# Part of the weight decoding moved from VectorE to GpSimd, another order of the first phase, and a check split in two

## The chip, the cores and the metric

The kernel runs on one core of a Trainium2 chip. A core has TensorE (matrix products into PSUM), VectorE and ScalarE (elementwise work on SBUF and PSUM), GpSimd (elementwise work on SBUF, and DMAs that it issues itself), SyncE, which here issues most DMAs, and 16 DMA engines. The metric is the device time in microseconds. Each engine works through its instructions in the order in which they were issued to it and waits for others by semaphores.

## The reference

A gated linear attention over four batches and eight heads, followed by a two-layer network with a squared ReLU:

```python
f = 1 / (1 + exp(-f_logit))                       # B=4, H=8, S=768, D=48
for t in range(S):
    state = f[:, :, t, :, None] * state + einsum('bhd,bhe->bhde', k[:, :, t], v[:, :, t])
    y[:, :, t] = einsum('bhd,bhde->bhe', q[:, :, t], state)
x = y.transpose(0, 2, 1, 3).reshape(3072, 384)    # tokens x model
h = maximum(x @ w_in, 0)                          # w_in 384 x 2048
out = (h * h) @ w_out                             # w_out 2048 x 384
```

The two weights arrive as 64-bit floats.

## The kernel before, in words

**Tiling.** The 768 steps are six blocks of 128, the eight heads four pairs. A *unit* is one block and one pair of heads; it is numbered block by block, so units 0 to 3 are block 0 and units 4 to 7 block 1. The network's 2048 hidden rows are 16 *pieces* f of 128. Of each piece there are two weights, one of `w_in` (called i0, i1, ...) and one of `w_out` (o0, o1, ...), each 128x384.

**A unit** goes through small stages, each a method with one letter: L loads gates, keys and queries (f and k load them apart), v loads the values, G takes the sigmoid on ScalarE, K the key scan on VectorE (line 422), in which GpSimd makes two 128x8 rows (line 427) that the query scan needs, Q the query scan (436), T and N transpose the keys (472 on TensorE, 478 on ScalarE), D and S are the state and score products (496, 507), M masks the scores (514), C forms the states (529, 534), r and s are crossed copies for the other half (458, 466), Y the output products (550, 562), H and X split the outputs into an upper and a lower part (575, 579). Heads have 48 rows of 64; the fourth pair lives in the rows that the other three leave free. So m moves 16 rows of a unit (447), and g and h bring the fourth pair's outputs into the other three's tiles (586), partly issued by GpSimd, partly by SyncE.

**Two-part products.** TensorE's single pass is of reduced width, so each operand is kept as an upper part and a lower part, and each product is three passes (line 251 for the up-projection, 277 for the down-projection): upper weight by lower x, lower weight by upper x, upper by upper. Nine passes of 512 columns make one up- or down-projection of a piece.

**Decoding.** A weight is loaded as 64-bit words and made into a 32-bit float: an absolute value and, for the pieces loaded early, a byte taken out by ScalarE (144, 148), two bit operations on VectorE (154, 161), and then the two parts: a copy that rounds to the upper part on ScalarE (176) and the subtraction that leaves the lower part on VectorE (178). In the order below these are the letters A I V c J for `w_in` and B O Z d P for `w_out`. The first six pieces (12 weights) are decoded *early*; the other ten later, while block 1's products run. A 112x256 piece, called w4, serves the fourth pair in pieces 0 and 1 and has the letters e n t a w.

**Phases.** The first phase computes block 0's units, block 1's units and pieces 0 to 5 of block 0's network; u and U are up-projections (u without the fourth pair's part for pieces 0 and 1, U0 and U1 then add that part), R and E the squaring and its lower part, W the down-projection. Then come all 16 pieces of block 1, the other ten pieces of block 0, and blocks 2 to 5, each with the next block's units between its pieces.

**What sets the order.** In the first phase two strings of such letters, FIRST and SECOND, are run through one after the other; each letter issues its instructions at once, and for the engines named in `manual_schedule` that order is kept. Before, these are TensorE, SyncE, VectorE and ScalarE; GpSimd's instructions are placed by the scheduler. The letters i, o, L, v issue loads on SyncE's queue. A load into a buffer that is still in use waits there, and all behind it on that queue.

**The verdict.** The fast decoding and the scans hold for a range of values. Near the end a check over all gate products and weights is made (`verdict`): four VectorE rows, a transpose on TensorE, three more VectorE rows. Its flag is read in the last block and decides whether a general path runs; with these inputs it doesn't. It is issued behind piece 12 of the last block but one.

Of the kernel before, what the change touches and what calls it, by code (L numbers as in the profile page):

```python
# [12 lines left out]
F32 = mybir.dt.float32  # L13
# [7 lines left out]
ALU = mybir.AluOpType  # L21
ET = mybir.EngineType
# [43 lines left out]
VERDICT_AT = 12  # L66
# [1 line left out]
SIGNED = ()  # L68

FIRST = """  # L70
f0 k0 L1 G0 K0 v0 o4 L2 Q0 busy11 T0 G1 N0 o0 K1 m0 busy3 S0 B4 j0 D0 i1 M0 r0 T1 C0 v1 G2 Q1 v2 s0
o5 busy2 Y0 B0 i5 K2 e0 m1 S1 v3 H0 i0 r1 n0 N1 Q2 o3 T2 B5 D1 L4 O0 r2 S2 M1 N2 C1 A0 D2 m2 t0 X0
D3 a0 v4 C2 s1 i3 I0 s2 Y1 A1 w0 V0 L5 Z0 G4 I1 S3 M2 H1 V1 r3 L6 X1 c1 C3 Y2 A3 K4 s3 v5 c0 v6 H2
M3 T4 o2 G5 X2 N4 J0 i2 Y3 A5 Q4 i4 d0 u0 H3 v7 P0 m4 r4 o1 X3 G6 I3 J1 A2 D4 K5
"""
SECOND = """
U0 A4 S4 I2 R0 T5 C4 u1 M4 s4 E0 N5 V2 Q5 Y4 c2 g3 h3 B1 U1 H4 W0 J2 m5 r5 X4 O1 R1 V3 Z1 D5 I4 S5
d1 E1 B3 U2 P1 C5 c3 B2 M5 W1 J3 s5 V4 K6 R2 Y5 c4 Q6 T6 H5 U3 N6 X5 m6 r6 J4 D6 R3 E2 S6 O2 U4 C6
Z2 s6 M6 d2 E3 Y6 R4 P2 I5 W2 V5 H6 E4 c5 X6 r7 J5 S7 O3 D7 M7 U5 C7 Z3 s7 O4 d3 Y7 Z4 P3 d4 W3 H7
P4 R5 X7 O5 g7 h7 Z5 W4 E5 d5 P5 W5  # L80
"""


class Moe:
# [28 lines left out]
    def decode_fourth(self):  # L113
        a = self.const.tile([P, DM], F32, tag=self.spare(), name="wa4")[:ROWS, : SPLIT * P]
        yield from self.bits(self.raw4, a, None, "j0")
        w = self.const.tile([P, 2, DM], F32R, tag=self.fourth_tag, name="w4")
        self.w4 = w[:ROWS, :, : SPLIT * P]
        yield from self.halves(self.w4, a)

    def decode(self, f, i, scr, early):  # L120

        if early:
            a = self.const.tile([P, DM], F32, tag=self.spare(), name=f"wa{f}_{i}")
        else:
            a = scr.tile([P, DM], F32, tag="wa", name=f"wa{f}_{i}", bufs=3)
        total = self.sums[:, 2 * f + i : 2 * f + i + 1]
        yield from self.bits(self.raw[f, i], a, total, f"{'io'[i]}{f}" if early else None)
        yield from self.parts(f, i, a)

    def bits(self, st, a, total, early):  # L130

# [35 lines left out]
            )  # L167
        yield

    def parts(self, f, i, a):  # L170
        self.w[f, i] = self.const.tile([P, 2, DM], F32R, tag=f"w{f}_{i}", name=f"w{f}_{i}")
        yield from self.halves(self.w[f, i], a)

    def halves(self, w, a):
        nc = self.nc
        nc.scalar.copy(out=w[:, 0], in_=a)  # L176
        yield
        nc.vector.tensor_tensor(out=w[:, 1], in0=a, in1=w[:, 0].bitcast(F32), op=ALU.subtract)  # L178
# [158 lines left out]
def fast_path(ctx, tc, moe, ident, low, fkqT, vN, w, w4, out):  # L337
    nc = tc.nc
# [340 lines left out]
    moe.begin(0, xs[0], half[0])  # L679
    early = ExitStack()  # L680
    pro = early.enter_context(tc.tile_pool(name="pro", bufs=1))
    with tc.manual_schedule(engines={ET.PE, ET.SP, ET.DVE, ET.Activation}):
        with tc.tile_pool(name="ps_p", bufs=2, space=bass.MemoryType.PSUM) as ps_p:
            for t in FIRST.split():
                step(t)
# [51 lines left out]
        for blk in range(2, NBLK):  # L737
# [8 lines left out]
                hook(0, first + out_at, 1, lambda un=un, stage=out_stage: un.stage(stage))  # L746

        general = []
        hook(len(order) - 2, VERDICT_AT, 1, lambda: general.append(verdict(nc, moe, low, ident, ps_a)))
        hook(  # L750
            len(order) - 1, VERDICT_AT, 1,
            lambda: general.append(nc.values_load(general[0][0:1, 0:1], min_val=0, max_val=1)),
        )
        for k, (blk, fs) in enumerate(order):
            if blk > 1 and blk + 1 < NBLK:
# [8 lines left out]
            else:  # L764
                moe.run(hooks[k])
                moe.finish(lambda e: out[blk, e * P : (e + 1) * P], None if blk else part)
    return general[1], obs


def verdict(nc, moe, low, ident, pool):  # L770
# [6 lines left out]
    nc.vector.tensor_scalar(out=moe.sums, in0=moe.sums, scalar1=MOST, scalar2=None, op0=ALU.is_lt)  # L777
    nc.vector.tensor_reduce(out=good[:, 1:2], in_=moe.sums, axis=mybir.AxisListType.X, op=ALU.min)
    nc.vector.tensor_tensor(out=good[:, 0:1], in0=good[:, 0:1], in1=good[:, 1:2], op=ALU.min)
    pl = pool.tile([1, P], F32, tag="pk", name="pl")  # L780
    nc.tensor.transpose(out=pl, in_=good[:, 0:1], identity=ident)
# [186 lines left out]
```

## Time and profile before

| what | us |
|---|---|
| median of three runs | 510.5 (509.83 to 512.45) |
| the profiled execution | 511.15, span 509.4 |
| TensorE busy in the span | 490.5 |
| VectorE busy | 263.0 |
| ScalarE busy | 284.0 |
| GpSimd busy | 29.2 |
| first phase, to the end of its last down-projection on TensorE | 76.3 |
| in it: TensorE, VectorE, ScalarE busy | 65.0, 65.8, 53.2 |

The profile is of one execution. In its views a row has its start and duration in microseconds, the engine, the line of the kernel, the operation and the tiles (output<-inputs); in brackets stands how long the engine sat idle before it and what ended that. PE is TensorE, PEld its weight loads, DVE VectorE, ACT ScalarE, POOL GpSimd, SPq SyncE's queue.

### The profile page before, as it was taken

To read this page: it belongs to the slowest core of one execution; us is meant where nothing else is said; L and a number is where in the kernel's file an instruction comes from. 1 tells how busy PE (TensorE), PEld (TensorE's weight loads), DVE (VectorE), ACT (ScalarE), POOL (GpSimd) and SP (SyncE) were. 2 spreads that over 40 slices of the span, in tenths; PEclk is the share of its full clock that TensorE was granted. 3 is DMA by queue.
4 is the path that set the end of the run, shared out by engine and by line. 5 is a ranking of instruction groups with operands and counts; after the bars stand their busy time and mean duration, and the time that the engine had idled before them with its cause. 6 is when DMAs were issued, how large, how long until landed. Compare 5 with 4: busy or idle time off the path is not lost.

```text
span 509.4 us, 11456 instructions
## 1 busy us (share of the span) xinstructions
PE 490.5 (96%) x4831; PEld 391.3 (77%) x4831; DVE 263.0 (52%) x483; ACT 284.0 (56%) x577; POOL 29.2 (6%) x66
## 2 busy tenths in 40 slices
PE   5799899999999999999999999999999999999996
PEld 5677677788777878777788787778777767888884
DVE  6899975989857335645324546224455241211112
ACT  3789746887757353755354754543656444544441
POOL 6112010001000000000000000000000000000000
PEclk9999999999999999999999999999999999999999
DMA  8992025562530206112005313004410001100001
GB/s 293 312 317 51 13 79 171 178 207 97 166 90 18 74 11 178 73 27 89 3 1 150 110 28 90 0 1 119 141 28 12 1 1 33 64 0 1 0 1 67
DMA packets 20364, 41.97 MB, mean 82 GB/s; under 512 B 2656, under 2 KB 5728, under 8 KB 20304
## 3 DMA queue, kind: packets, MB, share of 16 engines
q1 hardware_dynamic: 19856, 40.23, 26.0%
q0 software_dynamic: 448, 0.92, 0.8%
q8 instruction: 40, 0.66, 0.5%
q14 instruction: 20, 0.16, 0.1%
HBM read 31.69 MB, written 4.72 MB: 71 GB/s over the span
## 4 chain that ended last, share of the span: by engine, by line
PE 78%; DVE 12%; ACT 4%; DMA 3%; issue 2%; POOL 0%; SPq 0%; DVEq 0%; ACTq 0%; POOLq 0%
PE ph L251 36%; PE po L277 33%; PE ds L507 2%; PE ds L496 2%; PE py L550 2%; PE py L562 2%; DVE fkq L436 1%; DMA last_kq<-fkq 1%; DVE gl L268 1%; DVE fkq L422 1%; DMA fkq<-in_fkqT_dram 1%; DVE wa L161 1%; PE pk L472 1%; ACT ph L262 1%; DVE w L178 1%
## 5 line engine op out<-in xcount | busy, mean ns | idle before, releaser
L251 PE MATMUL ph<-x,w 128*128 128x512 f32 x864 | 222.4, 402 | 1.2 <-DVE gl L268 0.7
L251 PEld LDWEIGHTS ph<-x,w 128*128 128x128 f32 x864 | 160.0, 189 | 39.2 <-DVE gl L268 1.1
L277 PE MATMUL po<-gh,w 128*128 128x512 f32 x576 | 180.4, 394 | 0.3 <-DVE w L178 0.3
L268 DVE TENSOR_TENSOR gl<-ph,gh 128x512 fp32r<-128x512 f32 x96 | 66.2, 690 | 187.9 <-ACT gh L263 187.7
L261 ACT ACTIVATE ph<-ph 128x512 f32<-128x512 f32 x96 | 55.8, 582 | 136.6 <-PE ph L251 135.9
L277 PEld LDWEIGHTS po<-gh,w 128*128 128x128 f32 x576 | 108.1, 188 | 26.6 <-DVE w L178 0.6
L277 PE MATMUL po<-gl,w 128*128 128x512 f32 x288 | 114.7, 398 | 0.4 <-DVE gl L268 0.4
L277 PEld LDWEIGHTS po<-gl,w 128*128 128x128 f32 x288 | 54.1, 188 | 13.7 <-DVE gl L268 1.1
L263 ACT CAST gh<-ph 128x512 fp32r<-128x512 f32 x96 | 56.3, 586 | 3.0
L262 ACT ACTIVATE ph<-ph 128x512 f32<-128x512 f32 x96 | 55.9, 582 | 3.0
L427 POOL TENSOR_SCALAR fkq<-fkq 128x8 f32<-128x8 f32 x18 | 11.8, 656 | 324.0 <-DVE fkq L422 323.9
L422 DVE TENSOR_TENSOR_SCAN fkq<-fz,dr 128x520 f32<-128x520 f32 x18 | 22.3, 1237 | 6.7 <-ACT fz L417 6.6
L176 ACT CAST w<-wa 128x384 fp32r<-128x384 f32 (+1 forms) x33 | 16.8, 510 | 13.9 <-DVE wa L165 12.2
L550 PEld LDWEIGHTS py<-sc,vn 64*64 64x64 f32 (+1 forms) x640 | 18.0, 126 | 8.1 <-issue 7.0
L436 DVE TENSOR_TENSOR_SCAN fkq<-fz,dz 128x520 f32<-128x520 f32 x18 | 22.4, 1242 | 0.6
L550 PE MATMUL py<-sc,vn 64*64 64x64 f32 (+1 forms) x640 | 21.3, 222 | 0.7 <-DVE sc L514 0.7
L562 PE MATMUL py<-rx,sx 48*48 48x64 f32 (+1 forms) x320 | 20.7, 217 | 0.2
L514 DVE TENSOR_TENSOR sc<-ds,mask 128x512 f32<-128x512 f32 x24 | 16.5, 687 | 8.2 <-PE ds L507 7.5
L144 ACT ACTIVATE wa<-raw 128x384 f32<-128x384 f32 (+1 forms) x33 | 18.1, 549 | 4.5 <-DMA raw<-in_w_dram 4.4
L161 DVE SCALAR_TENSOR_TENSOR wa<-raw,wa 128x384 int32<-128x384 int32 (+1 forms) x33 | 18.1, 552 | 0.8
L562 PEld LDWEIGHTS py<-rx,sx 48*48 48x48 f32 (+1 forms) x320 | 18.1, 127 | 0.5 <-ACT sx L466 0.5
L178 DVE TENSOR_TENSOR w<-wa,w 128x384 fp32r<-128x384 f32 (+1 forms) x33 | 18.0, 546 | 0.7 <-ACT w L176 0.6
(93 smaller groups left out, 403.0 us busy)
## 6 DMA issues: line engine op xcount, KB each, us to landing
fkq<-in_fkqT_dram SPq DMA_DIRECT2D x17, 768.0 KB, 5.2
raw<-in_w_dram SPq DMA_DIRECT2D x32, 384.0 KB, 4.3
vn<-in_vN_dram SPq DMA_DIRECT2D x24, 192.0 KB, 4.9
out_dram<-ob SPq DMA_DIRECT2D x12, 256.0 KB, 2.1
x<-ys SPq DMA_DIRECT2D x30, 64.0 KB, 2.4
last_kq<-fkq SPq DMA_DIRECT2D x28, 64.5 KB, 2.3
out_dram<-part SPq DMA_DIRECT2D x3, 256.0 KB, 2.4
out_dram<-ob_last SPq DMA_DIRECT2D x3, 256.0 KB, 2.4
```

What stands on the lines that cost most here:

```text
L161: nc.vector.scalar_tensor_tensor(out=h, in0=upper, scalar=-(1 << 31), in1=h, op0=ALU.bitwise_and, op1=ALU.bitwise_or)
L178: nc.vector.tensor_tensor(out=w[:, 1], in0=a, in1=w[:, 0].bitcast(F32), op=ALU.subtract)
L251: self.nc.tensor.matmul(self.ph[f], lhsT=w[:, i], rhs=x[:, j], start=first and n == 0, stop=last and n == 2)
L261: nc.scalar.activation(ph, ph, AF.Relu)
L262: nc.scalar.activation(ph, ph, AF.Square)
L263: nc.scalar.copy(out=gh, in_=ph)
L268: self.nc.vector.tensor_tensor(out=gl, in0=self.ph.pop(f), in1=gh.bitcast(F32), op=ALU.subtract)
L277: self.nc.tensor.matmul(self.po[e], lhsT=l, rhs=r, start=f == self.fs[0] and i == 0, stop=f == self.fs[-1] and i == 2,)
L422: V.tensor_tensor_scan(out=rr[:, ::-1], data0=self.fz[:, NZ * CZ : 0 : -1], data1=dr[:, ::-1], initial=0.0, op0=ALU.mult, op1=ALU.add,)
L436: V.tensor_tensor_scan(out=pp, data0=self.fz[:, : NZ * CZ], data1=dz, initial=0.0, op0=ALU.mult, op1=ALU.add)
L550: nc.tensor.matmul(self.py[h * C : h * C + m, c, b * C : (b + 1) * C], lhsT=self.vn[rows, b, h * D : h * D + m], rhs=self.sc[rows, h, b], ...
L562: nc.tensor.matmul(self.py[h * C : h * C + m, c, b * C : (b + 1) * C], lhsT=s[rows, b * D : b * D + m], rhs=q[rows], start=False, stop=b = ...
```

## The change

Three things. The lower parts of the 12 early weights are computed by GpSimd instead of VectorE; those of w4 and of the later weights stay on VectorE. GpSimd's instructions now keep the written order too, and both strings of the first phase are new ones. And the verdict is issued in two steps, the first four VectorE rows behind piece 12, the rest from the transpose on behind piece 13.

```diff
-f0 k0 L1 G0 K0 v0 o4 L2 Q0 busy11 T0 G1 N0 o0 K1 m0 busy3 S0 B4 j0 D0 i1 M0 r0 T1 C0 v1 G2 Q1 v2 s0
+f0 k0 L1 G0 K0 i2 v0 o3 Q0 busy11 T0 L2 G1 N0 K1 m0 busy3 S0 r0 A2 i0 D0 M0 B3 v3 T1 C0 v1 Q1 s0 i1
...
     def decode_fourth(self):
...
-        yield from self.halves(self.w4, a)
+        yield from self.halves(self.w4, a, self.nc.vector)
...
     def decode(self, f, i, scr, early):
...
-        yield from self.parts(f, i, a)
+        yield from self.parts(f, i, a, self.nc.gpsimd if early else self.nc.vector)
...
-    def halves(self, w, a):
+    def halves(self, w, a, eng):
         nc = self.nc
         nc.scalar.copy(out=w[:, 0], in_=a)
         yield
-        nc.vector.tensor_tensor(out=w[:, 1], in0=a, in1=w[:, 0].bitcast(F32), op=ALU.subtract)
+        eng.tensor_tensor(out=w[:, 1], in0=a, in1=w[:, 0].bitcast(F32), op=ALU.subtract)
         yield
...
-    with tc.manual_schedule(engines={ET.PE, ET.SP, ET.DVE, ET.Activation}):
+    with tc.manual_schedule(engines={ET.PE, ET.SP, ET.DVE, ET.Activation, ET.Pool}):
...
-        hook(len(order) - 2, VERDICT_AT, 1, lambda: general.append(verdict(nc, moe, low, ident, ps_a)))
+        found = verdict(nc, moe, low, ident, ps_a)
+        for n in range(2):
+            hook(len(order) - 2, VERDICT_AT + n, 1, lambda: general.append(next(found)))
         hook(
             len(order) - 1, VERDICT_AT, 1,
-            lambda: general.append(nc.values_load(general[0][0:1, 0:1], min_val=0, max_val=1)),
+            lambda: general.append(nc.values_load(general[1][0:1, 0:1], min_val=0, max_val=1)),
         )
...
     nc.vector.tensor_tensor(out=good[:, 0:1], in0=good[:, 0:1], in1=good[:, 1:2], op=ALU.min)
+    yield
     pl = pool.tile([1, P], F32, tag="pk", name="pl")
...
-    return flag
+    yield flag
```

The loads ahead of unit 4's inputs (L4) in the order of issue were f0 k0 L1 v0 o4 L2 o0 j0 i1 v1 v2 o5 i5 v3 i0 o3; now they are f0 k0 L1 i2 v0 o3 L2 i0 v3 v1 i1 v2 j0 L5 v4 o4 i3 o0 L6.

Three places of the new order, as the instructions stand on an engine. In their names the number behind a tile is the buffer's; the digit of the piece is left out, so `w_0` is a piece of `w_in` and `w_1` one of `w_out`. First TensorE around unit 3's outputs and u0; before:

```order
L550 MATMUL first_py<-sc_3_529,vn_3_307 48x64 x4
L562 MATMUL first_py<-last_kq,sp_76 48x64
L562 MATMUL first_py<-rx_3_481,sx_78 48x64
L251 MATMUL ph_0_156<-x_0_115,w_0_524 128x512 x3
L251 MATMUL ph_0_156<-x_1_116,w_0_524 128x512 x3
L251 MATMUL ph_0_156<-x_2_117,w_0_524 128x512 x3
```

and now:

```order
L507 MATMUL ds_3_439<-last_kq 64x64 x16
L251 MATMUL ph_0_156<-x_0_115,w_0_497 128x512 x3
L251 MATMUL ph_0_156<-x_1_116,w_0_497 128x512 x3
L251 MATMUL ph_0_156<-x_2_117,w_0_497 128x512 x3
L550 MATMUL first_py<-sc_3_543,vn_3_233 48x64 x4
L562 MATMUL first_py<-last_kq,sp_76 48x64
```

u0 now follows unit 3's scores at once; unit 3's outputs and unit 4's transpose, which stood between them, come behind it.

Then ScalarE at unit 2's crossed states (the copy of `sp_75` to `sx_77`) and the upper part of i0, in the new order:

```order
L417 ACTIVATE fz_73<-fkq_1_307 128x8x64
L176 CAST w_0_431<-wa_0_330 128x384
L144 ACTIVATE wa_1_435,sums<-raw_1_344 128x384
L148 ACTIVATE raw_1_344<-raw_1_344,floor 128x384
L466 COPY sx_77<-sp_75 48x208
L144 ACTIVATE wa_1_462,sums<-raw_1_384 128x384
L148 ACTIVATE raw_1_384<-raw_1_384,floor 128x384
L458 COPY rx_3_492<-last_kq 48x256
L176 CAST w_0_497<-wa_0_310 128x384
```

Unit 5's gates and the words of o4 (`raw_1_344`) now stand ahead of the crossed states, and those of o0 (`raw_1_384`) and unit 3's queries ahead of the upper part of i0 (`w_0_497`); before, the crossed states followed those of unit 1 directly.

Last, GpSimd from unit 1's move on, in the new order:

```order
L447 DMA last_kq<-fkq_1_140 16x1032 x2
L178 TENSOR_TENSOR w_0_431<-wa_0_330,w_0_431 128x384
L178 TENSOR_TENSOR w_0_497<-wa_0_310,w_0_497 128x384
L178 TENSOR_TENSOR w_1_521<-wa_1_462,w_1_521 128x384
L427 TENSOR_SCALAR fkq_0_458<-fkq_0_458 128x8
L427 TENSOR_SCALAR low<-fkq_0_458 128x8
L447 DMA last_kq<-fkq_0_458 16x1032 x2
```

Three lower parts stand between unit 1's move and unit 4's rows; two follow unit 5's rows of line 427 and seven unit 6's.

More of the change, by code (lines that the diff above doesn't have):

```diff
@@ L70 @@
 FIRST = """
-f0 k0 L1 G0 K0 v0 o4 L2 Q0 busy11 T0 G1 N0 o0 K1 m0 busy3 S0 B4 j0 D0 i1 M0 r0 T1 C0 v1 G2 Q1 v2 s0
-o5 busy2 Y0 B0 i5 K2 e0 m1 S1 v3 H0 i0 r1 n0 N1 Q2 o3 T2 B5 D1 L4 O0 r2 S2 M1 N2 C1 A0 D2 m2 t0 X0
-D3 a0 v4 C2 s1 i3 I0 s2 Y1 A1 w0 V0 L5 Z0 G4 I1 S3 M2 H1 V1 r3 L6 X1 c1 C3 Y2 A3 K4 s3 v5 c0 v6 H2
-M3 T4 o2 G5 X2 N4 J0 i2 Y3 A5 Q4 i4 d0 u0 H3 v7 P0 m4 r4 o1 X3 G6 I3 J1 A2 D4 K5
+f0 k0 L1 G0 K0 i2 v0 o3 Q0 busy11 T0 L2 G1 N0 K1 m0 busy3 S0 r0 A2 i0 D0 M0 B3 v3 T1 C0 v1 Q1 s0 i1
+N1 Y0 G2 v2 j0 K2 m1 r1 S1 L5 H0 A0 D1 X0 A1 M1 T2 v4 C1 o4 Q2 s1 e0 busy2 Y1 i3 N2 o0 n0 m2 r2 I1
+S2 H1 L6 V1 G5 X1 D2 c1 M2 B4 J1 D3 C2 L4 I0 s2 B0 I2 Y2 t0 V0 r3 O0 o1 c0 Z0 S3 H2 J0 V2 v6 d0 X2
+o2 A3 P0 C3 u0 i5 M3 G4 I3 a0 K4 o5 s3 B1 Y3 i4 Q4 B2 v5 T4 v7 H3
 """
 SECOND = """
[L77 to L80, printed above, removed]
+u1 N4 X3 m4 B5 O2 w0 O1 r4 Z2 U0 g3 h3 Z1 c2 U1 K5 R0 J2 S4 D4 G6 E0 T5 d1 C4 W0 N5 P1 M4 s4 Q5 R1
+Y4 U2 H4 E1 m5 r5 X4 V3 A4 K6 S5 D5 R2 W1 C5 c3 J3 M5 s5 T6 Q6 A5 Y5 U3 H5 m6 r6 X5 E2 d2 I4 N6 S6
+P2 V4 R3 D6 M6 W2 C6 c4 E3 s6 J4 O5 r7 Y6 Z5 I5 d5 U4 V5 H6 P5 c5 X6 J5 O3 Z3 S7 R4 O4 D7 Z4 U5 C7
+d4 d3 P4 M7 s7 E4 P3 R5 Y7 W3 H7 E5 X7 g7 h7 W4 W5
 """
@@ L168, in bits, with parts @@
         yield
-    def parts(self, f, i, a):
+    def parts(self, f, i, a, eng):
         self.w[f, i] = self.const.tile([P, 2, DM], F32R, tag=f"w{f}_{i}", name=f"w{f}_{i}")
-        yield from self.halves(self.w[f, i], a)
-    def halves(self, w, a):
+        yield from self.halves(self.w[f, i], a, eng)
+    def halves(self, w, a, eng):
         nc = self.nc
@@ L196, in decode_any @@
         )
-        for _ in self.parts(f, i, a):
+        for _ in self.parts(f, i, a, self.nc.vector):
             pass
@@ L766, in fast_path @@
                 moe.finish(lambda e: out[blk, e * P : (e + 1) * P], None if blk else part)
-    return general[1], obs
+    return general[2], obs
 def verdict(nc, moe, low, ident, pool):
```

## The prediction

> **What bounds the kernel now.** I read the page first: the busy shares, then the forty slices.
>
> ```profile
> span 509.4 us, 11456 instructions
> PE 490.5 (96%) x4831; PEld 391.3 (77%) x4831; DVE 263.0 (52%) x483; ACT 284.0 (56%) x577; POOL 29.2 (6%) x66
> PE   5799899999999999999999999999999999999996
> DVE  6899975989857335645324546224455241211112
> DMA  8992025562530206112005313004410001100001
> ```
>
> TensorE sets the time: 490.5 of 509.4 us, full in every slice but the first three and the last. So only its 18.9 idle us, and its slow-clock time, can be won. Where they lie, the view by stretches tells; the cuts are at the end of unit 3's scores, the first up-projection u0, and the end of the last down-projection of the first phase (column two is the stretch, three is TensorE, five VectorE; the last is GB/s).
>
> ```profile
> 0.00:28.26 28.26, 19.71 (x380) 16.65 (x380) 22.57 (x43) 16.89 (x40) 9.98 (x26) 1.00 0.97 305
> 28.26:34.05 5.79, 4.97 (x101) 4.22 (x101) 5.65 (x11) 5.17 (x14) 0.97 (x2) 1.00 0.88 297
> 34.05:37.95 3.90, 3.90 (x15) 2.86 (x16) 3.87 (x7) 3.28 (x8) 1.04 (x3) 1.00 0.96 348
> 42.70:69.97 27.27, 25.35 (x520) 19.76 (x519) 25.91 (x51) 20.78 (x49) 2.66 (x6) 1.00 0.13 26
> 100.00:410.00 310.00, 309.45 (x3164) 246.99 (x3163) 160.12 (x281) 174.11 (x348) 11.15 (x24) 1.00 0.25 72
> 410.00:422.00 12.00, 10.75 (x47) 8.38 (x46) 4.18 (x14) 4.48 (x9) 0.00 (x0) 1.00 0.01 2
> ```
>
> Until 38 us the loads run at 0.88 to 0.97 of the DMA engines; from 42.7 to 70 VectorE is at 25.91 of 27.27 and TensorE loses 27.27 - 25.35 = 1.92 us. From 100 to 410 there is nothing to win (0.55), from 410 to 422 there is 1.25. The change touches the first 76 us and that last place.
>
> Then the chain of waits through the first 42 us, and TensorE's and ScalarE's rows there.
>
> ```profile
> 19.28 7.47 DMA last_kq<-fkq
> 26.89 1.37 PE ds L507 x32
> 34.12 3.84 PE ph L251 x9
> 94.82 2.10 PE ph L251 x9
> ```
> ```profile
> 24.66 0.34 PE L562 MATMUL first_py<-rx,sx 48*48 48x64 f32 x1 [1.24 <-ACT sx L466]
> 24.89 0.56 ACT L144 ACTIVATE wa<-raw 128x384 f32<-128x384 f32 x1
> 25.45 0.62 ACT L148 ACTIVATE raw<-raw,floor 128x384 int32<-128x384 uint8 x1
> 25.96 0.68 PE L562 MATMUL first_py<-rx,sx 48*48 48x64 f32 x2
> 26.34 0.63 ACT L417 ACTIVATE fz<-fkq 128x512 f32<-128x512 f32 x1 [0.27 <-DMA fkq<-in_fkqT_dram]
> 42.70 0.34 PE L550 MATMUL py<-sc,vn 64*64 64x64 f32 x8
> 43.79 0.95 PE L251 MATMUL ph<-ys,w 112*128 112x512 f32 x3
> 54.05 0.66 PE L472 MATMUL pk<-ident,fkq 128*128 128x128 f32 x4 [0.63 <-DVE fkq L428]
> ```
>
> Unit 3's scores wait for the 7.47 us that unit 2's rows take in the loaded queue. The nine products of u0 take 3.84 us, those of a later up-projection 2.10: u0 runs at half the rate.
>
> **The change, part by part.** *The verdict.* These rows are its place.
>
> ```profile
> 417.88 0.69 DVE L268 TENSOR_TENSOR gl<-ph,gh 128x512 fp32r<-128x512 f32 x1 [3.50 <-ACT gh L263]
> 418.49 0.29 DVE L774 TENSOR_REDUCE good<-low 128x1 f32<-128x144 f32 x1
> 419.12 0.16 DVE L779 TENSOR_TENSOR good<-good 128x1 f32<-128x1 f32 x1
> 419.34 0.27 PE L781 MATMUL pl<-ident,good 128*1 128x128 f32 x1 [1.25 <-DVE good L779]
> ```
>
> TensorE reaches the transpose while VectorE still ends the piece's lower part and the four verdict rows; it waits 1.25. A piece later, about 4 us of products lie between, and VectorE is done: the whole 1.25 goes. The consumer, the register load, stays fifteen pieces behind. **-1.25.**
>
> *The first phase's order.* I take the new order stage by stage with the durations above. Loads first; the page has their sizes.
>
> ```profile
> fkq<-in_fkqT_dram SPq DMA_DIRECT2D x17, 768.0 KB, 5.2
> raw<-in_w_dram SPq DMA_DIRECT2D x32, 384.0 KB, 4.3
> vn<-in_vN_dram SPq DMA_DIRECT2D x24, 192.0 KB, 4.9
> ```
>
> Adding these in the order of issue, unit 4's inputs end at 6.91 MB before and, with units 5 and 6 and a v ahead, at 8.68 MB now. They landed at 26.34; 1.77 MB more at 0.30 to 0.35 MB per us (297 and 348 GB/s above) is 5.1 to 5.9 us: 31.5 to 32. Piece o4's words now end at 6.32 MB, so some 2 us ahead of 26.3: 24.4. ScalarE decodes o4 (1.2 us, as 24.89 to 26.07) ahead of unit 2's crossed states, which so end near 26.2. Unit 2's outputs ended 25.96 + 0.68 - 24.66, about 1.8 us, after unit 1's states came: so 28.0, and unit 3's scores start there instead of at 26.89. That costs 1.1. Unit 2's rows leave VectorE later too (its first mask and states now stand ahead of its query scan, near 21.5 for 19.2), but 7.11 for 6.91 MB ahead of them in the queue would land them at 27.4, under that 28.0.
>
> Scores to 29.3; then u0, whose second product needs the lower part of piece i0 from GpSimd: ScalarE casts it behind o0's words (near 27) and unit 3's queries, to 29.1, GpSimd ends near 30.1, so u0 waits 0.4 and ends at 33.6. Before, unit 2's outputs, a wait, unit 4's transpose and unit 3's outputs came first and u0 ended at 37.95. Unit 3's outputs (1.1 at full clock, 42.70 to 43.79) to 34.7; unit 4's transpose needs its key scan, from 32.2 at best, 1.9 us (28.95 to 30.90 in the rows below): 34.1, so it ends at 35.4 unhindered. Then u1 to 37.5; the two fourth parts, the first of which waits for w4's lower part (still on VectorE, near 37.8), to 39.1; unit 4's scores and states to 40.4. Unit 5's transpose stands behind VectorE's key scan of unit 5, which follows five decode rows and ends near 41.1: TensorE idles 0.7 and is at 41.7. Before, all this but one fourth part was done at 42.70, with it at 43.4: **1.7 ahead.** Of this the half-rate clock gives most, since unit 3's outputs and the transpose come behind u0's 4 us.
>
> *GpSimd's lower parts.* Here the rows of VectorE from 42.7 to 71.2, grouped, then a row of the start and two places where both engines met.
>
> ```profile
> L178 DVE TENSOR_TENSOR w<-wa,w 128x384 fp32r<-128x384 f32 x8 | 4.4, 549 | 0.1
> ```
> ```profile
> 2.09 0.96 POOL L369 MEMSET last_kq<- 112x1040 f32 x1
> 30.26 0.74 POOL L427 TENSOR_SCALAR fkq<-fkq 128x8 f32<-128x8 f32 x1 [13.09 <-DVE fkq L422]
> 31.09 0.23 POOL L427 TENSOR_SCALAR low<-fkq 128x8 f32<-128x8 f32 x1
> 28.95 1.23 DVE L422 TENSOR_TENSOR_SCAN fkq<-fz,dr 128x520 f32<-128x520 f32 x1
> 30.21 0.69 DVE L428 TENSOR_TENSOR fkq<-fkq 128x512 f32<-128x512 f32 x1
> 30.82 0.68 DVE L514 TENSOR_TENSOR sc<-ds,mask 128x512 f32<-128x512 f32 x1
> 32.02 0.55 DVE L178 TENSOR_TENSOR w<-wa,w 128x384 fp32r<-128x384 f32 x1
> 32.49 0.20 DVE L434 RECIPROCAL dz<-fkq 128x8 f32<-128x8 f32 x1
> ```
>
> VectorE loses these eight rows, each 0.47 from the next (32.02 to 32.49), some 3.8 us, more than TensorE's 1.92 idle us in the same stretch. Walking the new order I still find about 0.5 us of waits there (unit 5's outputs behind its mask), so **1.4 ahead** more. No trace shows GpSimd doing such a row. Its fill of 1040 columns took 0.96, so 384 take 0.35 by width; with two inputs read in turn 0.7, and 0.23 as the short row has: 0.6 to 0.95. I take 0.9. GpSimd then works 12 x 0.9 = 11 us in 45, and up(f) finds its lower parts there except at u0. The Trainium skill, in "GPSIMD Engine Reference", section "Elementwise — side-by-side cycle accounting", has 2.6 cycles an element for two inputs at 1.2 GHz, an estimate of 0.83 us for 384; no run here shows it, and the sum would not move.
>
> What counts is what VectorE loses meanwhile. The 8-column row took 0.74 beside a VectorE row with both inputs in SBUF and ended 0.09 after it, and the same row beside a mask whose input is PSUM took 0.23: GpSimd waited. Whether VectorE also waits for GpSimd no row shows; the mask after it started on time. So the price per lower part on VectorE's chain lies between 0 (GpSimd always yields) and its whole 0.9, and nothing speaks for less than 0. I take 0.1, near the rows seen, because the lower parts mostly follow L427's rows, beside masks and states that read PSUM: 12 x 0.1 = **1.2 lost.** The Trainium skill's "SBUF — State Buffer", section "Who interferes with whom", says that the two share a port as a lock, that a VectorE instruction with two SBUF inputs contends with a GpSimd one that reads SBUF, and that whoever comes second waits for the whole of the first. The trace agrees for GpSimd's side (0.74 for 0.23); for the other side it is the first rival.
>
> *Sum.* 1.25 + 1.7 + 1.4 - 1.2 = 3.15 off the profiled execution's 511.15 (509.4 of span and 1.75 around it): 508.0. That execution is 0.65 above the median of the runs, so 510.5 - 3.15 = **507.4**. The next blocks and the tail stay: their order is not touched.
>
> **The rivals.** With p the price per lower part, the gain is 4.35 - 12p.
>
> *The port takes the gain.* GpSimd gets in between two VectorE rows and holds them off: at p from 0.15 to 0.57 the result lies within half a per cent (508 to 513); at p = 0.36 it is 510.5. For it: some two thirds of VectorE's time at 42 to 66 us is scans, decode rows and the like, both inputs in SBUF. Against: the new places beside PSUM rows. 24%.
>
> *The port at its full length*, the case on the other side. The place is the seven lower parts that GpSimd has in one file behind unit 6's L427, while VectorE decodes; if each stops VectorE for 0.6 to 0.9, the masks and lower parts that TensorE's outputs wait for come 3 to 6 us later than now. It decides from p = 0.57; at 0.9 the time is 510.5 - 4.35 + 10.8 = 517. Against: only if nearly every one meets a row with two SBUF inputs. 12%.
>
> *The loads take the gain.* Unit 4's inputs come behind 1.77 MB more. If they land at 33.5, key scan, transpose and unit 5's scan move 1.5 to 1.7 later, and 4.35 - 1.2 - 1.7 = 1.45 is left: 509. For it: DMA at 0.97 until 28 us. Against: units 5 and 6 are then in early. 14%.
>
> **How the numbers follow.** Half a per cent, 2.55 us, is about what a measurement here can tell from no change. The forecast has 50%, by itself 505 to 508 (p = 0 gives 506.2). Faster: 0.48 of it and 0.02 of the loads, 0.50. Same: 0.02 of it, 0.24 of the port, 0.12 of the loads, 0.38. Slower: 0.12. The range begins at 504.3 (p = 0 and all 1.9 us of leftover waits, 0.7 at unit 5's transpose, 0.5, and 0.7 at u0 and w4, gone too) and ends at 512.0, inside the first port case; beyond lie about 0.13 above and 0.05 below.
>
> **What would show it.** TensorE's wait at the verdict's transpose should be gone. u0 should start near 29.3 with a short wait for GpSimd's row, and end near 33.6; unit 4's gate row on ScalarE should begin near 32. L178's rows on GpSimd should be about 0.9 long, or 1.5 where they meet VectorE. The first phase's last down-projection should end near 74.4, for 76.3. VectorE rows with two SBUF inputs that take 1 us or more, or start late beside a GpSimd row, would prove the port rival; a gate row of unit 4 after 33 us the loads. The forecast is wrong if that end is not before 75.5.

## The result, and the profile after

| kernel | median, us | ratio to before, 95% interval | profiled execution's span |
|---|---|---|---|
| before, beside the change | 511.58 | 1 | 509.4 |
| the change | 515.16 (513.45 to 517.22) | 1.0074 [1.0050, 1.0098] | 513.1 |

The change makes the kernel slower by 0.74%, 3.8 us. The forecast was 507.4, faster, with a range that ended at 512.0. Times differ by some tenths between the sets of runs below, so kernels of different sets are compared by their ratios to the kernel before.

The page of the changed kernel: span, busy shares, and the slices of TensorE and DMA.

```profile
span 513.1 us, 11465 instructions
PE 489.3 (95%) x4831; PEld 390.0 (76%) x4831; DVE 262.6 (51%) x471; ACT 284.4 (55%) x577; POOL 42.7 (8%) x78
PE   5878879999999999999999999999999999999996
DMA  8792107265502305412004412003510001100001
```

TensorE has lost time in its third to sixth slices (7, 8, 8, 7 tenths for the 9, 9, 8, 9 of before), that is from 26 to 77 us. Nothing is lost behind them: the products that follow the first phase's last down-projection begin at 81.18 in the profiled execution, for 76.15 before, 5.0 later, and the verdict gives 1.25 back, which makes the 3.7 by which the spans differ. VectorE is as busy as before, though twelve instructions were taken from it. Both facts point at VectorE in the first phase.

TensorE's waits, longest first: what it waited for, us in total, times, the longest. Behind them stands the wait of the same output products (550) in the kernel before.

```profile
PE first_py L562 <- ACT sx L466: 2.9, 1, 2.9
PE pk L472 <- DVE fkq L428: 2.9, 2, 2.1
PE py L550 <- DVE sc L514: 2.3, 1, 2.3
PE py L550 <- DVE dz L434: 2.1, 2, 1.3
PE ph L649 <- POOL ident masks.py:199: 1.6, 1, 1.6
PE ds L507 <- DVE fkq L439: 1.4, 3, 0.8
PE py L550 <- DVE state L534: 1.1, 1, 1.1
PE ds L507 <- DMA last_kq<-fkq: 1.0, 1, 1.0
```
```profile
PE py L550 <- DVE sc L514: 0.7, 1, 0.7
```

The verdict's transpose is gone from the list. The waits of the transposes for the key scan (472) and of the first products at the start (649) were there before too, with 3.3 and 1.6. Two have grown most. The wait for crossed states (line 562 for 466) is 2.9, for 1.4 before, and belongs to the second loss below. The output products (550) wait 5.5 in all for VectorE's masks, reciprocals and states, for 0.7 before. How one of these comes about stands in the timelines of VectorE, GpSimd and TensorE at 53 to 57 us.

```profile
53.42 0.35 DVE L529 TENSOR_TENSOR sp<-state,fkq 112x192 f32<-112x192 f32 x1
54.26 1.19 DVE L529 TENSOR_TENSOR sp<-state,fkq 112x192 f32<-112x192 f32 x1
55.76 0.68 DVE L514 TENSOR_TENSOR sc<-ds,mask 128x512 f32<-128x512 f32 x1
56.36 0.20 DVE L434 RECIPROCAL dz<-fkq 128x8 f32<-128x8 f32 x1
54.23 1.01 POOL L178 TENSOR_TENSOR w<-wa,w 128x384 fp32r<-128x384 f32 x1 [0.33 <-ACT w L176]
56.59 0.34 PE L550 MATMUL py<-sc,vn 64*64 64x64 f32 x8 [1.33 <-DVE dz L434]
```

The same VectorE row takes 0.35 at 53.42, with GpSimd elsewhere, and 1.19 at 54.26, when it starts 0.03 behind a lower part on GpSimd; it ends at 55.45, 0.21 after the GpSimd row does (55.24). Mask and reciprocal come 0.84 later by it, and TensorE stands 1.33 for them. The groups of VectorE's rows from 42 to 74 us say how often this happens. Columns behind the shapes: count, busy us, mean ns of one, idle us before them. First the change, then the same code with the lower parts back on VectorE (the second experiment).

```profile
L161 DVE SCALAR_TENSOR_TENSOR wa<-raw,wa 128x384 int32<-128x384 int32 x7 | 5.3, 751 | 0.2
L529 DVE TENSOR_TENSOR sp<-state,fkq 112x192 f32<-112x192 f32 x6 | 4.8, 792 | 0.1
L529 DVE TENSOR_TENSOR sp<-state,last_kq 112x192 f32<-112x192 f32 x2 | 1.4, 712 | 0.0
```
```profile
L161 DVE SCALAR_TENSOR_TENSOR wa<-raw,wa 128x384 int32<-128x384 int32 x7 | 3.9, 555 | 0.1
L529 DVE TENSOR_TENSOR sp<-state,fkq 112x192 f32<-112x192 f32 x6 | 2.1, 353 | 0.1
L529 DVE TENSOR_TENSOR sp<-state,last_kq 112x192 f32<-112x192 f32 x2 | 0.7, 354 | 0.0
L178 DVE TENSOR_TENSOR w<-wa,w 128x384 fp32r<-128x384 f32 x9 | 5.0, 550 | 0.0
```

The rows of the three groups grow by 1.4 + 2.7 + 0.7 = 4.8 us. All three read two inputs from SBUF (so do the scans and lines 154, 428 and 439). The nine lower parts that VectorE does in that stretch otherwise take it 5.0, or 9 x 0.47 = 4.2 from one to the next: what was taken from VectorE is all spent on waiting. Rows with one input in PSUM keep their length. The mask's at 72.85 starts within the second of two rows of GpSimd, and no mask of the 24 is longer than the others (shortest, median and longest ns):

```profile
71.34 2.06 POOL L178 TENSOR_TENSOR w<-wa,w 128x384 fp32r<-128x384 f32 x2 [2.10 <-ACT w L176]
71.47 1.07 DVE L529 TENSOR_TENSOR sp<-state,last_kq 112x192 f32<-112x192 f32 x1
72.85 0.68 DVE L514 TENSOR_TENSOR sc<-ds,mask 128x512 f32<-128x512 f32 x1
L514 DVE TENSOR_TENSOR sc<-ds,mask x24: 676/691/692, 12.1 to 414.7; 128x512 f32<-128x512 f32 x24
```

The second loss is earlier. SyncE's queue (SPq), the move that GpSimd issues, and on ScalarE unit 5's gates, unit 2's crossed states and unit 4's gates, in the change:

```profile
10.83 0.34 SPq L653 DMA_DIRECT2D raw<-in_w_dram  x1
19.30 0.55 SPq L410 DMA_DIRECT2D fkq<-in_fkqT_dram  x1
12.35 1.19 POOL L447 DMA_DIRECT2D last_kq<-fkq  x2
24.85 0.63 ACT L417 ACTIVATE fz<-fkq 128x512 f32<-128x512 f32 x1 [2.40 <-DMA fkq<-in_fkqT_dram]
27.44 0.36 ACT L466 COPY sx<-sp 48x208 f32<-48x208 f32 x1
34.51 0.63 ACT L417 ACTIVATE fz<-fkq 128x512 f32<-128x512 f32 x1 [1.04 <-DMA fkq<-in_fkqT_dram]
```
```profile
SPq L410 <- DMA last_kq<-fkq: 7.9, 2, 7.8
```

SyncE's queue issues nothing from 10.83 to 19.30. It stands at unit 5's load, whose buffer is the one that unit 0 leaves, and that is free only when unit 0's 16 rows have been moved out of it. GpSimd issues that move at 12.35, behind unit 1's two short rows, because GpSimd now keeps the written order and the new string has m0 behind K1. In the kernel before it was at 9.18:

```profile
9.18 1.17 POOL L447 DMA_DIRECT2D last_kq<-fkq  x2 [2.23 <-DVE fkq L439]
```

All loads behind unit 5's come late by that, unit 4's among them; its gates begin at 34.51. Unit 5's own load matters sooner. ScalarE stands 2.40 for it at unit 5's gates, and unit 2's crossed states, which the new order has behind these gates, follow at 27.44. They are what TensorE waits 2.9 for, its longest single wait, and u0 starts at 31.81, for the 29.3 of the forecast.

### The profile page after: what moved, and what is told of

The parts are those of the page before. It is cut to its first block, busy times and chain, and to the rows that moved or that the text cites. A ratio compares the mean times of both kernels' runs of the same rounds, so it can differ in the third digit from the quotient of the medians.

```text
span 513.1 us, 11465 instructions
## 1 busy us (share of the span) xinstructions
PE 489.3 (95%) x4831; PEld 390.0 (76%) x4831; DVE 262.6 (51%) x471; ACT 284.4 (55%) x577; POOL 42.7 (8%) x78
## 4 chain that ended last, share of the span: by engine, by line
PE 75%; DVE 12%; DMA 4%; ACT 4%; issue 1%; SPq 1%; POOL 1%; DVEq 0%; ACTq 0%; POOLq 0%
PE ph L251 34%; PE po L277 33%; DMA fkq<-in_fkqT_dram 3%; PE py L550 2%; DVE wa L161 2%; PE ds L496 2%; PE py L562 2%; PE ds L507 2%; DVE gl L268 1%; DVE fkq L422 1%; DVE sp L529 1%; DVE fkq L436 1%; DMA last_kq<-fkq 1%; PE pk L472 1%; ACT ph L262 1%
## 5 line engine op out<-in xcount | busy, mean ns | idle before, releaser
L427 POOL TENSOR_SCALAR fkq<-fkq 128x8 f32<-128x8 f32 x18 | 12.3, 683 | 314.6 <-DVE fkq L422 314.5
L514 DVE TENSOR_TENSOR sc<-ds,mask 128x512 f32<-128x512 f32 x24 | 16.5, 687 | 7.7 <-PE ds L507 7.5
L161 DVE SCALAR_TENSOR_TENSOR wa<-raw,wa 128x384 int32<-128x384 int32 (+1 forms) x33 | 19.4, 595 | 1.0
L466 ACT COPY sx<-sp 48x208 f32<-48x208 f32 x44 | 16.0, 364 | 4.3 <-DVE sp L529 3.1
```

Of the source, the lines that this page charges most:

```text
L161: nc.vector.scalar_tensor_tensor(out=h, in0=upper, scalar=-(1 << 31), in1=h, op0=ALU.bitwise_and, op1=ALU.bitwise_or)
```

## The experiments

Each was timed against the kernel before on its own chip; "ratio" is to that kernel, with its 95% interval.

**The verdict alone.** The kernel before with the verdict in two steps and nothing else.

```diff
-        hook(len(order) - 2, VERDICT_AT, 1, lambda: general.append(verdict(nc, moe, low, ident, ps_a)))
+        found = verdict(nc, moe, low, ident, ps_a)
+        for n in range(2):
+            hook(len(order) - 2, VERDICT_AT + n, 1, lambda: general.append(next(found)))
```

> The kernel before with the verdict in two steps and nothing else. Both theories (the port between VectorE and GpSimd, and the loads held up on SyncE's queue) lie in the first phase and say nothing against it: TensorE's 1.25 us wait ahead of the verdict's transpose goes, and the time is 1.25 us (0.24%) below before's. If the wait only moves a piece on, no change.

Measured: 510.41, ratio 0.9983 [0.9969, 0.9998], span 508.1, which is 1.3 under 509.4. In ratios it is 0.9 us, with an interval from 0.1 to 1.6; the term of 1.25 stands.

**The lower parts back on VectorE**, in the new order and with the new verdict.

```diff
-        yield from self.parts(f, i, a, self.nc.gpsimd if early else self.nc.vector)
+        yield from self.parts(f, i, a, self.nc.vector)
```

> The changed kernel, its order and two-step verdict, but with the early lower parts on VectorE again. Port theory: the VectorE rows that took 1.07 to 1.25 us instead of 0.35 to 0.56 go back, about 4.9 us in all between 44 and 73 us, while nine lower parts at 0.47 (4.2 us) come back to VectorE there: 0.5 to 1 us below the changed kernel, so still some 2.5 to 3 us above before. Loads theory: unit 4's gates still begin near 34.5 us, and the time is within 1 us of the changed kernel's. A third, that GpSimd's rows themselves cost the time: the time falls to before's or, with the verdict, 1.2 below.

Measured: 513.47, ratio 1.0044 [1.0024, 1.0063]. The stretched rows are gone (the groups above), but only 0.3% comes back (0.5 to 1 us had been expected), since VectorE now does the nine rows itself. So this run shows the net of the move, about 1.5 us to the bad by the midpoints (the two intervals overlap), and not the price of GpSimd's rows alone. It also shows that the new order, without GpSimd's help, is slower than the old one by 0.6% (1.0044 against 0.9983 for the verdict alone). By this comparison GpSimd's rows are a third of the change's loss, and the rest needs another cause.

**The old order, with GpSimd's lower parts.** The changed code with the two strings of before.

> The changed kernel with the two strings of the kernel before: lower parts on GpSimd in the old order, verdict in two steps. Port theory: each lower part takes 0.47 off VectorE and stretches another row of it by some 0.4, so VectorE is no freer and the first phase ends where it did, 76 +- 1 us; with the verdict about 1.2 below before. Loads theory: the loads stand as before, unit 4's gates near 26.3 us: also about 1.2 below. If the port alone carries the loss (4.9 us), the first phase ends near 80 us and the time is 3 us above before.

Measured: 510.57, ratio 0.9995 [0.9981, 1.0009]. Beside the verdict alone (0.9983) the lower parts on GpSimd bring nothing, and by the midpoints lose 0.6 us, within both intervals; 1.2 us below before had been expected, and 0.25 came. VectorE's rows with two SBUF inputs are stretched there too, from 30 to 76 us, as the groups show: by 6 x (578 - 353) = 1.35 us, 9 x (593 - 551) = 0.4, and 3 x (1116 - 692) = 1.3 for line 439, with 0.6 more for line 428. That is 3.6 us, not much under the 4.8 of the change. So the sum of the stretch is not what TensorE loses: it depends on what waits for the stretched rows. In this order the 12 lower parts taken from VectorE (12 x 0.47 = 5.6) and the stretch leave it freer by 2, and the time does not show it.

```profile
L529 DVE TENSOR_TENSOR sp<-state,fkq 112x192 f32<-112x192 f32 x6 | 3.5, 578 | 0.1
L154 DVE SCALAR_TENSOR_TENSOR wa<-wa,raw 128x384 int32<-128x384 int32 x9 | 5.3, 593 | 0.0
L161 DVE SCALAR_TENSOR_TENSOR wa<-raw,wa 128x384 int32<-128x384 int32 x9 | 4.9, 552 | 0.1
L439 DVE TENSOR_TENSOR fkq<-fkq 128x512 f32<-128x512 f32 x3 | 3.3, 1116 | 0.1
```

**GpSimd writes but reads nothing.** The change, with each of the 12 rows on GpSimd turned into a fill of the same tile with zeros. Order, waits and tiles stay; the row takes 0.42 instead of 1.04.

```diff
+        if eng is nc.gpsimd:
+            nc.gpsimd.memset(w[:, 1].bitcast(F32), 0.0)
+        else:
             eng.tensor_tensor(out=w[:, 1], in0=a, in1=w[:, 0].bitcast(F32), op=ALU.subtract)
```

> The changed kernel, but GpSimd fills the 12 early lower parts with zeros instead of subtracting (so the early weights' lower parts are left out of the products): its rows write and read nothing. Port theory, by reads: VectorE's stretched rows (1.07 to 1.25 us) are back at 0.35 and 0.55, and the time falls by 2 to 3 us, below the run with the lower parts on VectorE, since nobody pays for them. If a write holds VectorE off as well, the rows stay stretched, by a shorter time (0.35 to 0.45 a fill), and less than 1.5 us is won. Loads theory: unit 4's gates stay near 34.5.

Measured: 509.21, ratio 0.9954 [0.9939, 0.9969]. Its groups of VectorE from 42 to 74 us (the edit shifts line 529 to 532), and TensorE's rows of u0, of unit 5's transpose, and of the first products behind the phase (251 and 472 are 254 and 475). Below them stand the last two rows as the change has them.

```profile
L161 DVE SCALAR_TENSOR_TENSOR wa<-raw,wa 128x384 int32<-128x384 int32 x6 | 3.3, 556 | 0.2
L532 DVE TENSOR_TENSOR sp<-state,fkq 112x192 f32<-112x192 f32 x6 | 2.1, 355 | 0.1
29.67 4.21 PE L254 MATMUL ph<-x,w 128*128 128x512 f32 x9
42.14 0.63 PE L475 MATMUL pk<-ident,fkq 128*128 128x128 f32 x4 [0.80 <-DVE fkq L431]
74.65 4.35 PE L254 MATMUL ph<-x,w 128*128 128x512 f32 x18
```
```profile
44.30 0.63 PE L472 MATMUL pk<-ident,fkq 128*128 128x128 f32 x4 [0.80 <-DVE fkq L428]
81.18 4.35 PE L251 MATMUL ph<-x,w 128*128 128x512 f32 x18
```

No row is stretched, though three of line 532 start within a fill (42.51, 51.12 and 65.66 us), and from the change to this kernel the time falls by 1.2%, 6.1 us with an uncertainty of about 1.4 from the two intervals, where 2 to 3 had been expected. For 12 rows that is 0.5 us each. Part of it could be the fill's shorter length; but TensorE's and its weight loads' waits for GpSimd's rows in the change were 0.4 and 0.5 us, once each, so that share is small. Behind the phase both kernels take the same (513.1 - 81.18 and 506.8 - 74.65, both 432 us), so the zeros in the weights gain nothing there. The Trainium skill, in "SBUF — State Buffer", section "Who interferes with whom", states that a VectorE instruction with two SBUF inputs contends with a GpSimd instruction that reads SBUF and not with one that only writes it. These two kernels agree: 792 and 355 ns for the same group.

The profiled executions say where the 6.1 lie. From unit 5's transpose, ahead of the first stretched row (44.68), to the products behind the phase TensorE takes 36.9 in the change and 32.5 here: 4.4 us, about the stretch of 4.8. With the lower parts on VectorE (the second experiment) it is 35.7. The waits of the output products (550) go the same way: 5.5 in the change, 3.0 with the lower parts on VectorE, 1.2 with fills. The other 2 us lie ahead of that transpose (44.30 for 42.14), where no row of VectorE is stretched. Ahead of all lower parts GpSimd's row behind unit 1's inputs is already 1.2 later in the change's execution (11.31 for 10.11). That those 2 us belong to GpSimd's reads is not shown; without them the price is 4.4 / 12 = 0.37 per lower part.

**Unit 0's move ahead of unit 1's key scan**, which frees unit 5's buffer earlier.

```diff
-f0 k0 L1 G0 K0 i2 v0 o3 Q0 busy11 T0 L2 G1 N0 K1 m0 busy3 S0 r0 A2 i0 D0 M0 B3 v3 T1 C0 v1 Q1 s0 i1
+f0 k0 L1 G0 K0 i2 v0 o3 Q0 busy11 T0 L2 G1 N0 m0 K1 busy3 S0 r0 A2 i0 D0 M0 B3 v3 T1 C0 v1 Q1 s0 i1
```

> The changed kernel with one instruction pair moved: GpSimd issues unit 0's move ahead of unit 1's two rows of line 427 (as the kernel before did, at 9.2 us) instead of behind them (12.4). Loads theory, as it now stands: unit 5's load waits on SyncE's queue for that move, so it is issued 3 us sooner (near 16 for 19.3), the DMA engines are not left at 0.77 between 10 and 20 us, unit 4's gates begin near 31.5 for 34.5 and the time falls by 2 to 3 us, to within 1.5 us of before. Port theory alone, or the order's other parts: at most 0.7 us.

> The same with the early lower parts on VectorE: the new order, its queue no longer held, GpSimd without lower parts. If loads (about 2.5 us) and port (1.5, from 1.0074 against 1.0044) add, the time is 4 us below the changed kernel, some 0.5 below before. If the port costs nothing once the loads come in time, it is no faster than the run with the move alone.

Measured: with GpSimd's lower parts 514.32, ratio 1.0050 [1.0031, 1.0069]; with them on VectorE 512.31, ratio 1.0011 [1.0001, 1.0022]. GpSimd issues the move at 9.19, unit 5's load leaves at 16.5 and 16.0, and unit 4's gates begin at 32.06 and 31.86. Against the kernels without the edit (1.0074 and 1.0044) that is 0.24% and 0.33%, 1.2 and 1.7 us. The intervals of the second pair do not meet, those of the first do. From the first kernel 2 to 3 us had been expected; the second was to be 4 us below the change and is 3.2. ScalarE no longer stands at unit 5's gates (23.19 in the first kernel), and u0 starts at 30.15 for 31.81. So the held queue is a second cause, of 1 to 2 us. Between these two kernels the lower parts on GpSimd cost 2.0 us (1.0050 against 1.0011, intervals apart), which makes the net of the move clearer than the first pair did. The second of these kernels is still 0.28% above the verdict alone: with early loads and VectorE's own lower parts the new order remains a little worse than the old.

**Unit 4's load in unit 5's place**, unit 5's behind m2; then also their gates exchanged; then that with the lower parts on VectorE.

```diff
-... m1 r1 S1 L5 H0 ... n0 m2 r2 I1 ... G5 X1 ... L4 I0 ... G4 I3 ...
+... m1 r1 S1 L4 H0 ... n0 m2 L5 r2 I1 ... G5 X1 ... I0 ... G4 I3 ...
+... m1 r1 S1 L4 H0 ... n0 m2 L5 r2 I1 ... G4 X1 ... I0 ... G5 I3 ...
```

> The changed kernel with one exchange on SyncE's queue: unit 4's load, whose buffer is free, takes the place of unit 5's, which waited from 11.2 to 19.3 us for a buffer; unit 5's stands behind unit 2's move. Loads theory: the queue isn't held up, unit 4's gates begin before 31 us (34.5 in the changed kernel), unit 4's key scan 3 to 4 us sooner, and the time falls by 2.5 to 3.5 us, to about before's. Port theory alone: the stretched VectorE rows stay (about 4.9 us in sum), unit 5 comes later, and the time falls by 1 us at most.

> As the run that exchanged the loads of units 4 and 5, which was slower because ScalarE stood 6.7 us at unit 5's gates with unit 2's crossed states behind it; now the gates of units 4 and 5 are exchanged too. Loads theory: ScalarE is not held, unit 2's crossed states come near 26 us, unit 4's key scan is no longer waiting for its load but for VectorE's rows ahead of it, and the time falls to 2 to 4 us below the changed kernel. If unit 5's inputs are what the chain needs, it stays near the changed kernel.

> The run with unit 4's load and gates first (513.33), but with the lower parts of the first six pieces back on VectorE. If GpSimd's reading holds VectorE off for about what VectorE saves by giving a lower part away (0.5 us lost, 0.47 saved), this move is worth what it was worth in the other two pairs: 1.3 to 2.0 us, so 511.3 to 512, ratio 0.999 to 1.001, and the 112x192 subtractions from two SBUF inputs are back at 0.35. If the new order was held back by unit 4's late inputs alone, what is left of it must show here, with those inputs early and no GpSimd row in the way: 508 to 509.5, ratio under 0.997, below the run that has the verdict alone.

Measured: 517.95, ratio 1.0134 [1.0107, 1.0161], for the first. This was a miss: unit 5's gates stand ahead of unit 4's on ScalarE, and ScalarE, which takes its rows in order, stood there.

```profile
28.65 0.63 ACT L417 ACTIVATE fz<-fkq 128x512 f32<-128x512 f32 x1 [6.69 <-DMA fkq<-in_fkqT_dram]
```

With the gates exchanged too, 513.33, ratio 1.0024 [1.0007, 1.0041]; unit 4's gates begin at 23.11, eleven us before those of the change, and still the kernel is slower than before. Early inputs alone don't mend it. With the lower parts on VectorE as well, 511.48, ratio 1.0007 [0.9991, 1.0024], 0.9 us less by the midpoints, for 1.3 to 2.0 expected, and the intervals overlap. In this pair's profiled executions TensorE takes 36.8 us with GpSimd and 37.1 with VectorE from unit 5's transpose to the end of the phase, so they don't show where the gain lies. The other theory of that run, that the new order shows its worth once loads and GpSimd are out of the way, fell: it is not under the verdict alone.

**Shorter rows on GpSimd.** If GpSimd holds VectorE for the length of one of its instructions, shorter instructions hold it for less. Each lower part as two rows of 192 columns; as four of 96 (with the early move of unit 0); and as two in the old order.

```diff
-        eng.tensor_tensor(out=w[:, 1], in0=a, in1=w[:, 0].bitcast(F32), op=ALU.subtract)
+        if eng is nc.gpsimd:
+            for c in (slice(0, DM // 2), slice(DM // 2, DM)):
+                eng.tensor_tensor(out=w[:, 1, c], in0=a[:, c], in1=w[:, 0, c].bitcast(F32), op=ALU.subtract)
+        else:
+            eng.tensor_tensor(out=w[:, 1], in0=a, in1=w[:, 0].bitcast(F32), op=ALU.subtract)
```

> The change, with each lower part on GpSimd written as two rows of 192 columns. If GpSimd holds VectorE off for one instruction at a time, the longest a VectorE row is stretched falls from 0.70 to 0.85 to some 0.35 to 0.5: the 112x192 subtractions take at most 0.85 and the decode rows at most 1.05, no row of these kinds is at 1.1 or over, and the time is 0 to 2 us below the change's 515.16 (0 if the second half of each row meets the next VectorE row just as the first did, so that the sum of stretch stays near 4.9). If VectorE stands for as long as GpSimd has such rows queued, the stretched rows stay at 1.1 to 1.25 and the time at 515 or, with 12 more rows' fixed cost, 516.

> The change with unit 0's move ahead of unit 1's key scan, and each lower part on GpSimd as four rows of 96 columns. The early move was worth 1.2 us, the halves 3.0. If one GpSimd instruction at a time holds VectorE off, a row of 96 columns holds it for about 0.25 at most, the 112x192 subtractions stay under 0.65 and the decode rows under 0.85, and the gains add up: 0.997 to 1.000, 509.5 to 511. If each meeting costs a fixed time beside the length, or GpSimd's 48 rows get too long in all for the products that wait for them, it is no better than the halves were: 1.001 to 1.003.

> The kernel before with its own order, the verdict in two steps, and the early lower parts on GpSimd as two rows of 192 columns each. If what GpSimd's rows cost is the length of one of its instructions at each meeting, the halves give back what the whole rows took in this order (0.9995 with them, 0.9983 without, so 0.6 us): 0.997 to 0.9985, 509.5 to 510.3, with no stretched row above 0.85. If the loss in this order was another one (a lower part that came late for a product, as 70.54 showed, 0.7 us), the halves change nothing: 0.9990 to 1.0000.

Measured: halves 512.17, ratio 1.0014 [0.9998, 1.0030]; quarters with the early move 510.73, ratio 0.9982 [0.9965, 0.9999]; halves in the old order 509.91, ratio 0.9964 [0.9950, 0.9979]. The rows of GpSimd and of VectorE's line 529 over the whole program (533 in the split kernels), as counts and shortest, median and longest ns; first the change, then halves, then quarters.

```profile
L178 POOL TENSOR_TENSOR w<-wa,w x12: 995/1040/1458, 26.0 to 72.3; 128x384 fp32r<-128x384 f32 x12
L529 DVE TENSOR_TENSOR sp<-state,fkq x30: 342/357/1194, 44.7 to 400.9; 112x192 f32<-112x192 f32 x30
```
```profile
L180 POOL TENSOR_TENSOR w<-wa,w x24: 580/642/1267, 25.3 to 71.5; 128x192 fp32r<-128x192 f32 x24
L533 DVE TENSOR_TENSOR sp<-state,fkq x30: 346/357/787, 44.7 to 399.0; 112x192 f32<-112x192 f32 x30
```
```profile
L180 POOL TENSOR_TENSOR w<-wa,w x48: 381/392/1317, 24.1 to 70.4; 128x96 fp32r<-128x96 f32 x48
L533 DVE TENSOR_TENSOR sp<-state,fkq x30: 348/357/585, 43.2 to 396.4; 112x192 f32<-112x192 f32 x30
```

The longest row of VectorE is 0.84, 0.43 and 0.23 us above its median of 0.357; the median row of GpSimd is 1.04, 0.64 and 0.39. For this row the longest hold is the length of one GpSimd row less about 0.2 (0.20, 0.21, 0.16). The theory that VectorE stands for as long as GpSimd has such rows queued is out: one instruction at a time holds it. The time follows: halves are 0.60% under the change, 3.1 us, more than the 0 to 2 expected; with the early move, quarters are 0.68% under whole rows (0.9982 for 1.0050). From unit 5's transpose to the end of the phase TensorE takes 34.9 with halves and 33.8 with quarters, between the 36.9 of whole rows (with the early move too) and the 32.5 of fills. The quarters also answer what the fills left open: reading rows of 0.39 still hold VectorE, fills of 0.42 don't, so the fills' shorter length isn't why they hold nothing up.

Halves in the old order make the fastest complete kernel here. Its VectorE groups from 42 to 74 us, with the products behind the phase:

```profile
L533 DVE TENSOR_TENSOR sp<-state,fkq 112x192 f32<-112x192 f32 x5 | 2.1, 419 | 0.1
L161 DVE SCALAR_TENSOR_TENSOR wa<-raw,wa 128x384 int32<-128x384 int32 x9 | 5.4, 613 | 0.1
76.50 4.36 PE L255 MATMUL ph<-x,w 128*128 128x512 f32 x18
```

It beats the kernel before (0.9964, the whole interval under 1) and the change. That it beats the verdict alone isn't shown: the intervals overlap, and in the profiled executions the phase ends at 76.50 here and 76.34 there, with spans of 508.4 and 508.1. No stretched row above 0.85 us had been expected; those of lines 428 and 439, which take 0.69 alone, reach 0.91, and one of line 154 reaches 0.95.

## Why the prediction was wrong, point by point

**The verdict: right.** 1.25 was forecast; the span fell by 1.3 with that part alone, the time by 0.9 in ratios.

**GpSimd's row: right in length, wrong in what it does to VectorE.** 0.9 was assumed, 1.04 measured. The wait of u0 for its lower part, 0.4, came as forecast (TensorE waited 0.4 for a GpSimd row, once, within u0). The step that failed is the price per lower part, "I take 0.1, near the rows seen, because the lower parts mostly follow L427's rows, beside masks and states that read PSUM". From the change to the kernel whose GpSimd rows read nothing, the price is 6.1 / 12 = 0.5 us by ratios; by TensorE's time behind unit 5's transpose it is 4.4 / 12 = 0.37, near the stretch of VectorE's rows there (4.8 in all). With 1.2 forecast, that is 4.9 or 3.2 us of the miss. The rows from which 0.1 was drawn were too few and had one direction only: a GpSimd row that came second and waited. Nothing in them spoke of a VectorE row that comes second. The argument from PSUM was half right: masks and the second rows of the states (534) read PSUM and kept their length. But each state has a first row, 529, with both inputs in SBUF, and that one makes 3.4 of the 4.8 us.

**So it was the first rival, with its price in the upper half of its range.** The prediction bounded p by 0 and 0.9 and had the port take the gain at 0.15 to 0.57; 0.37 and 0.5 fall there. That rival's own formula, 4.35 - 12p, gives no gain at 0.37 and a loss of 1.7 at 0.5, 510.6 to 512.2; the time was slower than that, since the 4.35 was too large as well. Its mark, "VectorE rows with two SBUF inputs that take 1 us or more", is in the trace six times (1.07 to 1.25, the scans left out, which take 1.24 with no GpSimd row beside them).

**The order: walked nearly right without GpSimd's reads, its gain too large.** With fills the stages come 0.4 to 1.6 us behind the forecast's walk through them: u0 at 29.67 for 29.3, unit 5's transposed keys at 42.77 for 41.7, the phase's end at 74.8 for 73.2 (the forecast end of 74.4 without its 1.2). In ratios the gain was 0.46%, 2.35 us, for the 4.35 of the terms at p = 0, so 2.0 are missing. The step that the runs show to be wrong here is the loads'. It counted bytes at 0.30 to 0.35 MB per us and never asked whether SyncE's queue could issue them: unit 5's load waited 7.8 us for unit 0's buffer, and the new place of m0 behind K1 on GpSimd made that longer. The walk let ScalarE go through to unit 2's crossed states without a wait, to end near 26.2; ScalarE stood 2.40 for unit 5's load, and the crossed states ended at 27.8. Putting the move back brought their end to 26.6 and unit 4's gates to 32.06 (near 32 was forecast), and was worth 1.2 to 1.7. Loads were one of the rivals, and "a gate row of unit 4 after 33 us" is there (34.51), but by another mechanism than more bytes. A part of the 34.51 is only that execution's: unit 1's inputs landed later in it than in the six other kernels with the same string up to there (GpSimd's row behind them at 11.31, for 10.11 to 11.15).

**The sum.** The miss is 3.15 + 3.8 = 6.9 us. By ratios 4.9 of it come from the price of a lower part and 2.0 from the order and its loads, each with an uncertainty of about 1.4 us. The profiled execution of the change is as far behind the walk, its phase ending at 81.3 for 74.4, but splits otherwise. By the end of unit 5's transpose it is 3.2 behind (44.93 for 41.7), ahead of all stretched rows, and 3.7 more come later, of which the price of the lower parts makes 4.4 - 1.2 = 3.2. So the price of a lower part is 3.2 to 4.9 of the miss, and the order with its loads the rest.

**What stays open.** Where in these ranges the two shares lie isn't settled. With the lower parts on VectorE and the early move, the new order is 0.28% slower than the old with the same verdict. Whether the rest is VectorE's load, for which the new order wasn't made, or something else in the order, was not told apart. Nor was it told apart why halves in the old order have a lower median than the verdict alone.

## What to carry to other kernels

In these runs an elementwise instruction that was moved to an idle GpSimd wasn't free for VectorE. For each VectorE row with two SBUF inputs that may meet it, count nearly the whole length of the moved row as the most it may cost (0.84 of 1.04 here), then ask what waits for that VectorE row; rows with an input in PSUM didn't pay. If the work has to go there, cut it into shorter instructions, since the hold was one instruction long. Work that only writes, as a fill does, was the better candidate: it held up nothing. Where a transfer's time is summed from bytes, first look what its queue stands at: a load for a buffer that another engine's DMA has yet to empty holds all loads behind it, and an engine that reads that load holds its own later rows.

## What the runs showed of the hardware that was not expected

A VectorE row with two SBUF inputs that starts within a GpSimd row with two SBUF inputs ends behind that row, the later the longer it is itself: in the change and in the old order by 0.21 to 0.22 us where it takes 0.35 alone (up to 1.19), by 0.41 to 0.42 where it takes 0.56 (up to 1.25), and by 0.55 where it takes 0.69 (up to 1.33, in the old order). Each time that is its own length less about 0.14. Two such rows kept their length (at 26.02 in the change, at 64.38 in the old order), and there GpSimd's row was the long one, 1.46 and 1.78. The hold falls with the length of GpSimd's row: 0.84, 0.43 and 0.23 us for rows of 1.04, 0.64 and 0.39. GpSimd's fills of 128x384 (0.42 us each) hold no such row up; three start within one and take 0.35 to 0.36. VectorE rows with one input in PSUM aren't held either: two masks, three second rows of the states (534) and two splits (579) start within GpSimd's rows in the change and keep their 0.68, 0.35 and 0.69. On GpSimd itself a row of 384 columns takes 1.04 and two of 192 take 1.28, four of 96 take 1.57: cutting costs GpSimd 0.24 and 0.53 us per lower part, and still the kernel gains.
